# A TensorE order with an empty GpSimd instruction as the relay between two row tiles

## The chip, the cores and the metric

The kernel runs on one core of a Trainium2 chip. The metric is the device time of one execution in microseconds, median over runs. The engines are TensorE (PE, with its weight loads PEld), VectorE (DVE), ScalarE (ACT), GpSimd (POOL) and SyncE (SP, which issues most DMAs).

## What is computed

A token-wise gate mixes an attention block and a gated feed-forward block of the same input, in float32. There are 2048 tokens of width 512, 32 query heads of width 16 that share one key head and one value head, and a hidden width of 1376.

```python
g = sigmoid((x * gate_w).sum(-1, keepdims=True))
q = (x @ wq) split into 32 heads;  k = x @ wk;  v = x @ wv
a = concat_heads(softmax(q @ k.T * 16**-0.5) @ v) @ wo
b = (gelu(x @ w_gate) * (x @ w_up)) @ w_down
out = g * a + (1 - g) * b
```

## The kernel before

A first part (82 us) loads the inputs, computes keys, values and all queries, writes the queries to a scratch tensor in HBM, and does the first feed-forward chunks. Then comes one long stretch (1147 us) in which attention and feed-forward are interleaved on TensorE, and a short end (15.5 us) for the last output projection.

In the long stretch TensorE's program order is written out by hand, in `PLAN`: 78 lines, one for each feed-forward or output-projection job (the first line has none), with steps that `play` (called at the end of `mix_kernel`) turns into instructions:

- **S** and **Z**: one score pair (`scores`, L751): two matmuls on the two row tiles (rows 0 to 50 and 64 to 114 of the array), each 512 columns, into one PSUM area of two banks; then ScalarE's exp over 128x1024 into a buffer `p` (L754, 12 buffers). S uses area 0 or 1 in turn, Z uses area 2, which `z` of a job holds between H and R. There are 1024 of them.
- **V**: one step of probabilities times values (`pv`, L821): eight matmuls on four column tiles of 32, over all 128 rows. It needs the `p` of two scores. There are 512.
- **H**: opens a job with two accumulators, `z` in area 2 and `y` in a bank of its own.
- **F**: one pair of matmuls of the job (`pair_mm`, L519), one for z and one for y, 512 columns each, on the two row tiles of 64 rows at the same time. A gate job has 24 F (`gate_job`), a down job or output job 12, 18 or 24.
- **R**: closes the job and issues its VectorE work; **T** issues the tanh of the gelu on ScalarE.

A contraction over 128 rows is split over the two row tiles. In half 0 of a job z uses the rows 0 to 63 and y the rows 64 to 127; in half 1 they change places. So the bank of z passes from one row tile to the other in the middle of the job, and the matmuls of half 1 may not start before those of half 0 have ended. `pair_mm` secures that with a relay: an instruction on GpSimd (L527) that waits for the last F of half 0 and that the first F of half 1 waits for. The steps that stand in PLAN between the 12th and the 13th of 24 F run meanwhile. In the whole list the half change holds these steps:

| steps in the half change | jobs before |
|---|---|
| S V S | 43 |
| S V V S | 17 |
| S V V S S | 7 |
| others with V | 9 |
| S S | 1 |

`split` (L201, L202) divides weights and inputs into a high part (VectorE, L201) and a low part (GpSimd's subtraction, L202). Its work is put into `slot` calls between the F, and it shares GpSimd's queue with the relay. `score`, `visit`, `norm` and `advance` issue further loads, normalisation and gelu steps as the list goes on.

Of the kernel before, what the change touches and what calls it, by code (L numbers as in the profile page):

```python
# [9 lines left out]
F32 = mybir.dt.float32  # L10
# [10 lines left out]
S = 2048  # L21
D = 512
H = 32
DH = 16
F = 1376
# [17 lines left out]
PB = 12  # L43
PLAN = [
# [78 lines left out]
]  # L123


# [1 line left out]
def mix_kernel(ctx, tc, xT, wq, wo, wf, out):  # L127
    nc = tc.nc
    cp = ctx.enter_context(tc.tile_pool(name="cp", bufs=1))
# [363 lines left out]
    def slot(split_too):  # L493
        for q in (todo, lazy, bg) if split_too else (bg,):
            if q:
                return q.pop(0)()
# [7 lines left out]
            nc.tensor.matmul(ps, a, b, start=(first and q == 0), stop=(last and q == len(terms) - 1),  # L504
                             skip_group_check=True)

    mark = cp.tile([1, 1], F32, name="mark")
    SYNC = mybir.DependencyInfo(mybir.DependencyClass.Sync, mybir.DependencyReason.DATA)

    def after(ins, name):  # L510
        tc.add_manual_dep(ins, name, SYNC, reason="a bank passes from one row tile to the other")

    def pair_mm(z, y, X, Y):
        for half in range(2):
            for q in range(len(X)):
                for j, (ps, (a, b)) in enumerate(((z, X[q]), (y, Y[q]))):
                    lower = (j + half) % 2
                    rs = slice(64 * lower, 64 * lower + 64)
                    mm = nc.tensor.matmul(ps, a[rs], b[rs], start=(half == 0 and q == 0),  # L519
                                          stop=(half == 1 and q == len(X) - 1), skip_group_check=True)  # L520
                    if half == 1 and q == 0:
                        after(mm.ins, relay[0])
                    if half == 0 and q == 0 and j == 0:
                        behind = [None, None]
                    behind[j] = mm.ins.name
                if half == 0 and q == len(X) - 1:
                    relay = nc.gpsimd.memset(mark, 0.0).ins  # L527
                    for name in behind:
                        after(relay, name)
                    relay = [relay.name]  # L530
                if q % EVERY == EVERY - 1 and (half == 0 or q + 4 <= len(X)):
                    slot(half == 1 or q + 6 <= len(X))
                yield
# [403 lines left out]
```

## Time and profile before

| | |
|---|---|
| median of 3 runs | 1246.28 us (1244.94 to 1249.26) |
| profiled execution, its own time | 1246.9 us |
| span of its trace | 1244.8 us |
| TensorE, ScalarE, VectorE, GpSimd busy | 99%, 83%, 42%, 17% |
| granted TensorE clock, mean | 0.999 |

The page gives busy shares and the chain of work that ended last. TensorE's matmuls overlap, so that the sum of their durations is no measure; the prediction goes by differences of their starts, which the order of time shows to 0.01 us.

### The profile page before, as it was taken

What the parts mean: (1) busy time and instruction counts of PE and PEld (TensorE: products, weight loads), DVE (VectorE), ACT (ScalarE), POOL (GpSimd) and SP (SyncE); (2) the same over time, 40 slices, a digit from 0 to 9 for tenths busy, and PEclk for the clock granted to TensorE, in tenths of its full rate; (3) what the DMA queues carried; (4) which work ended last, traced back from release to release, by engine and by line L of the source; (5) the groups of instructions that cost most, each with busy time, mean ns of one, the idle gap of its engine ahead of it and who ended that gap; (6) DMA issues with size and microseconds to landing.
All of it is one profiled execution on the core that took longest, in us unless ns stands there. A gap on an engine that the chain in (4) does not pass through costs nothing.

```text
span 1244.8 us, 23618 instructions
## 1 busy us (share of the span) xinstructions
PE 1237.2 (99%) x9742; PEld 657.5 (53%) x9742; DVE 526.2 (42%) x844; ACT 1031.7 (83%) x1127; POOL 215.6 (17%) x265
## 2 busy tenths in 40 slices
PE   9999999999999999999999999999999999999998
PEld 6775555454544554545454555554544555455544
DVE  7872553525423144443443234162455126253334
ACT  5448888988888888888888788888889888898894
POOL 5420311212210120211230021120231011121100
PEclk9999999999999999999999999999999999999999
DMA  8541201103201211101210221010211201010000
GB/s 329 193 149 43 83 14 65 40 23 107 73 15 31 70 40 40 65 24 40 89 53 14 74 65 40 14 65 16 92 58 40 74 14 65 14 58 34 14 1 34
DMA packets 28317, 73.89 MB, mean 59 GB/s; under 512 B 4208, under 2 KB 4464, under 8 KB 28208
## 3 DMA queue, kind: packets, MB, share of 16 engines
q1 hardware_dynamic: 27664, 71.32, 17.1%
q8 instruction: 77, 1.26, 0.4%
q0 software_dynamic: 256, 0.79, 0.2%
q10 hardware_dynamic: 288, 0.26, 0.1%
q14 instruction: 32, 0.26, 0.1%
HBM read 57.41 MB, written 14.94 MB: 58 GB/s over the span
## 4 chain that ended last, share of the span: by engine, by line
PE 92%; issue 1%; POOL 0%; DVE 0%; ACT 0%; DMA 0%; SPq 0%; POOLq 0%
PE acc L821 38%; PE s L751 23%; PE y L519 17%; PE z L519 13%; PE wos L504 1%; POOL xl L202 0%; DVE acc L634 0%; DMA Q<-scr 0%; PE wof L504 0%; ACT p L754 0%; SPq L364 0%; ACT sq L551 0%; SPq L363 0%; POOLq L202 0%; POOL mark L527 0%
## 5 line engine op out<-in xcount | busy, mean ns | idle before, releaser
L754 ACT ACTIVATE p<-s 128x1024 f32<-128x1024 f32 x1024 | 977.4, 1026 | 150.3 <-PE s L751 139.7
L821 PE MATMUL acc<-p,v 128*32 128x512 f32 x4096 | 496.4, 599 | 0.0
L751 PE MATMUL s<-Q,kp 51*128 51x512 f32 x2048 | 397.2, 421 | 1.0 <-DMA Q<-scr 0.9
L751 PEld LDWEIGHTS s<-Q,kp 51*128 51x128 f32 x2048 | 183.7, 184 | 258.0 <-ACT p L754 167.3
L821 PEld LDWEIGHTS acc<-p,v 128*32 128x32 f32 x4096 | 106.7, 109 | 239.2 <-issue 231.2
L527 POOL MEMSET mark<- 1x1 f32 x77 | 7.6, 99 | 890.0 <-PE y L519 874.0
L519 PE MATMUL z<-xh,gh 64*128 64x512 f32 x312 | 122.9, 394 | 0.0
L519 PE MATMUL y<-xh,gh 64*128 64x512 f32 x312 | 122.8, 394 | 0.0
L519 PE MATMUL z<-xl,gh 64*128 64x512 f32 x312 | 122.2, 392 | 0.3 <-POOL xl L202 0.2
L519 PE MATMUL y<-xl,gh 64*128 64x512 f32 x312 | 122.4, 392 | 0.0
L544 DVE COPY gs<-z 128x512 f32<-128x512 f32 x39 | 27.0, 692 | 225.4 <-PE z L519 214.9
L519 PE MATMUL z<-xh,gl 64*128 64x512 f32 x312 | 121.9, 391 | 0.0
L519 PE MATMUL y<-xh,gl 64*128 64x512 f32 x312 | 121.9, 391 | 0.0
L202 POOL TENSOR_TENSOR gl<-st,gh 128x512 fp32r<-128x512 f32 x80 | 107.4, 1361 | 36.5 <-DVE gh L201 35.7
L624 DVE SCALAR_TENSOR_TENSOR acc<-z,gc,acc 128x512 f32<-128x512 f32 x24 | 18.0, 751 | 130.9 <-PE z L519 128.3
L519 PE MATMUL z<-dh,hh 64*128 64x512 f32 x176 | 69.2, 393 | 0.0
L519 PE MATMUL y<-dh,hh 64*128 64x512 f32 x176 | 69.1, 393 | 0.0
L519 PE MATMUL y<-dl,hh 64*128 64x512 f32 x176 | 68.9, 392 | 0.0
L519 PE MATMUL z<-dl,hh 64*128 64x512 f32 x176 | 68.9, 391 | 0.0
L519 PE MATMUL z<-dh,hl 64*128 64x512 f32 x176 | 68.8, 391 | 0.0
L519 PE MATMUL y<-dh,hl 64*128 64x512 f32 x176 | 68.7, 391 | 0.0
L519 PEld LDWEIGHTS y<-xh,gl 64*128 64x128 f32 x312 | 57.7, 185 | 8.4
(174 smaller groups left out, 1536.9 us busy)
## 6 DMA issues: line engine op xcount, KB each, us to landing
st<-wf SPq DMA_DIRECT2D x40, 768.0 KB
scr<-q SPq DMA_DIRECT2D x16, 512.0 KB
Q<-scr SPq DMA_DIRECT2D x64, 128.0 KB
Q<-scr SPq DMA_DIRECT2D x64, 64.0 KB
out<-acc SPq DMA_DIRECT2D x16, 256.0 KB
xr<-xT SPq DMA_DIRECT2D x6, 512.0 KB
xst<-xT SPq DMA_DIRECT2D x12, 256.0 KB
st<-wf SPq DMA_DIRECT2D x5, 256.0 KB
```

Source lines behind the costliest of these rows:

```text
L202: eng_l.tensor_sub(lo, src, hi)
L504: nc.tensor.matmul(ps, a, b, start=(first and q == 0), stop=(last and q == len(terms) - 1), skip_group_check=True)
L519: mm = nc.tensor.matmul(ps, a[rs], b[rs], start=(half == 0 and q == 0), stop=(half == 1 and q == len(X) - 1), skip_group_check=True)
L527: relay = nc.gpsimd.memset(mark, 0.0).ins
L544: nc.vector.tensor_copy(gs, g)
L624: nc.vector.scalar_tensor_tensor(o, ps, w, o, op0=ALU.mult, op1=ALU.add)
L751: nc.tensor.matmul(ps[:, j * TG : (j + 1) * TG], kp[rs, kc * P : (kc + 1) * P], Q[u][rs, pr], start=True, stop=True)
L754: nc.scalar.activation(p, ps, AF.Exp, bias=0.0, scale=SCALE)
L821: nc.tensor.matmul(accp[u][32 * j : 32 * j + 32], vt[:, kc], pb[s, j // 2][:, (j % 2) * TG : (j % 2 + 1) * TG], start=(kc == 0), stop=(kc ...
```

## The change

The relay's instruction becomes an empty one instead of a memset of one element, and the tile `mark`, which only the memset wrote, goes. Its dependencies stay as they are. Beside it all 77 job lines of PLAN are replaced by a new order of the same steps; five of them are shown here. A V group is a run of V with nothing between. In numbers: F 1608 and 1608, S and Z together 1024 and 1024 (119 Z before, 148 after), V 512 and 512, V groups 275 and 245. The half change holds S S in 52 jobs after, S V S in 13, one S in 5, and others with V in 7.

```diff
 PLAN = [
     "t: S2",
-    "f: H F6 S F3 S F3 S V S F S F5 S F3 S F3 R S V S Z T S V2 Z S V2 S",
-    "f: H F3 S F3 S F3 S V S F2 S F6 S F R S V2 S Z S V3 S",
-    "f: H F3 S F3 S F3 S V2 S F3 S F4 S F2 R S V2 S",
-    "f: H F S F5 S F3 S F3 S V S F3 S F3 S F3 S F3 R S V S Z T S V4 Z S2 V2 S",
-    "f: H F3 S F3 S F3 S F3 S V S F S F5 S F3 S F3 R S V Z S T S V4 S Z S V2 S",
...
+    "f: H F6 S F6 S2 F6 S F4 S F2 R S V S Z T S V3 Z S2 V2 S",
+    "f: H F3 S F3 S F3 S V S F S F6 S F2 R S V S Z S V3 S Z S V2 S",
+    "f: H F3 S F6 S2 F6 S F3 R S V S Z S V2 S",
+    "f: H F3 S F3 S F3 S F3 S V2 S F2 S F4 S F3 S F3 R S V Z S T S V4 S Z S V2 S",
+    "f: H F3 S F3 S F6 S2 F6 S F3 S F3 R S V Z S T S V4 S Z S V2 S",
...
 ]
...
-    mark = cp.tile([1, 1], F32, name="mark")
     SYNC = mybir.DependencyInfo(mybir.DependencyClass.Sync, mybir.DependencyReason.DATA)
...
                 if half == 0 and q == len(X) - 1:
-                    relay = nc.gpsimd.memset(mark, 0.0).ins
+                    relay = nc.gpsimd.nop(nofuse=True).ins
                     for name in behind:
                         after(relay, name)
                     relay = [relay.name]
```

144 rows, old and new, of the table PLAN are left out of this document.

## The prediction

> **What bounds the kernel now.** I read the page first: busy shares, granted clock, chain. Then the busy time by stretch, then the order of time on TensorE at single hand-overs, last the views of the GpSimd relay.
>
> ```profile
> span 1244.8 us, 23618 instructions
> ...
> PE 1237.2 (99%) x9742; PEld 657.5 (53%) x9742; DVE 526.2 (42%) x844; ACT 1031.7 (83%) x1127; POOL 215.6 (17%) x265
> ...
> PE 92%; issue 1%; POOL 0%; DVE 0%; ACT 0%; DMA 0%; SPq 0%; POOLq 0%
> PE acc L821 38%; PE s L751 23%; PE y L519 17%; PE z L519 13%; PE wos L504 1%; POOL xl L202 0%; DVE acc L634 0%; DMA Q<-scr 0%; PE wof L504 0%; ACT p L754 0%; SPq L364 0%; ACT sq L551 0%; SPq L363 0%; POOLq L202 0%; POOL mark L527 0%
> ```
> ```profile
> 0.00:82.20 82.20, 78.96 (x334) 60.61 (x334) 64.57 (x108) 35.84 (x62) 33.66 (x55) 1.00 0.63 233
> 82.20:1229.30 1147.10, 1146.67 (x9360) 587.98 (x9360) 450.60 (x717) 995.84 (x1065) 181.91 (x211) 1.00 0.15 47
> 1229.30:1244.80 15.50, 11.62 (x52) 8.94 (x48) 11.05 (x20) 0.00 (x0) 0.00 (x0) 0.94 0.18 68
> ```
>
> The chain lies 92% on TensorE. The second row of the stretches (columns: stretch, its length, then busy us of PE, PEld, DVE, ACT, POOL) is the part that PLAN orders: 1147.1 us, in which TensorE is without an instruction for 0.4 us, at full granted clock. The 82.2 us ahead of it and the 15.5 us behind it hold nothing that the diff touches. So the time is the sum of TensorE's steps in the list's order, and a new order is worth what it changes in the steps' prices. Busy time can't show those, since matmuls overlap; starts can. One hand-over of a gate job, TensorE alone:
>
> ```profile
> 142.15 0.40 PE L519 MATMUL z<-xh,gh 64*128 64x512 f32 x1
> ...
> 142.62 0.39 PE L519 MATMUL z<-xh,gl 64*128 64x512 f32 x1
> ...
> 142.85 0.41 PE L751 MATMUL s<-Q,kp 51*128 51x512 f32 x2
> 143.19 1.07 PE L821 MATMUL acc<-p,v 128*32 128x512 f32 x8
> 144.18 0.50 PE L751 MATMUL s<-Q,kp 51*128 51x512 f32 x2
> 144.52 0.39 PE L519 MATMUL y<-xh,gh 64*128 64x512 f32 x1
> ...
> 144.76 0.39 PE L751 MATMUL s<-Q,kp 51*128 51x512 f32 x2
> 144.99 0.39 PE L519 MATMUL y<-xl,gh 64*128 64x512 f32 x1
> ```
> ```profile
> 150.30 3.57 PE acc L821 x32
> ...
> 387.50 2.71 PE acc L821 x24
> ```
>
> An F is a pair z, y on the two row tiles, an S one score pair, a V eight matmuls on L821. Three F and their switch to S take 142.85 - 142.15 = 0.70, so 0.233 us each; S to F beside no V is 144.99 - 144.76 = 0.23. The second fence, pieces of the chain, has groups of four V and of three: a further V costs 3.57 - 2.71 = 0.86. Around a V group three steps are longer: S to V 143.19 - 142.85 = 0.34 (0.11 over 0.23); V to S 0.99 (0.13 over 0.86, and 3.57 - 4 x 0.86 gives the same 0.13); the S behind it 144.52 - 144.18 = 0.34 (0.11 over). **A V group costs 0.35 us beyond its work**, whatever its length.
>
> The check is the whole stretch. PLAN holds 1608 F, 1024 S (Z included), 512 V, and V stand in 275 groups. 2632 x 0.233 + 512 x 0.86 = 613.3 + 440.3 = 1053.6; the rest of the 1147.1 is 93.5 us, or 0.34 for each of 275 groups. So these prices explain the stretch, waits are a few us at most, and 0.34 is what I use (0.35 is rounding and a little of other waits the other way).
>
> **The list.** Counted in the diff: F, S and V are as many as before, V groups are 245 instead of 275. 30 x 0.34 = 10.2 us leave TensorE, on the path, with nothing to hide them. Where they come from: of the 77 jobs the half change (last F of half 0 to first F of half 1) holds V in 76 before, 43 of them S V S. After it holds S2 in 52, one S in 5, V in 20. The V taken out join groups elsewhere. Five V follow an F directly, which the trace doesn't show; between no surcharge and one more of 0.11 that is 0.5 us either way, and I take the price of S to V, as F and S cost each other nothing.
>
> **The hand-over.** S V S gives the relay 0.34 + 0.99 + 0.34 us, so none of those 76 is seen to stall. S2 gives 0.46 us. The trace has S2 once, with the memset:
>
> ```profile
> 817.06 0.39 PE L519 MATMUL z<-xh,gl 64*128 64x512 f32 x1
> ...
> 817.29 0.68 PE L751 MATMUL s<-Q,kp 51*128 51x512 f32 x4
> ...
> 817.58 0.15 POOL L527 MEMSET mark<- 1x1 f32 x1 [8.74 <-PE y L519]
> ...
> 817.78 0.18 PEld L519 LDWEIGHTS z<-xh,gh 64*128 64x128 f32 x1
> ...
> 817.81 0.47 PE L519 MATMUL y<-xh,gh 64*128 64x512 f32 x1
> ...
> 818.12 0.39 PE L519 MATMUL z<-xl,gh 64*128 64x512 f32 x1
> ```
> ```profile
> L527 POOL MEMSET mark<- x77: 88/88/381, 86.8 to 1219.2; 1x1 f32 x77
> L527 POOLq EVENT_SEMAPHORE  x76: 17/17/17, 101.5 to 1219.1; - x76
> its engine sat idle before it (us, times) until:
>   PE y L519: 874.0, 75
>   PE s L751: 15.9, 1
> ```
>
> The last pair of half 0 ends at 817.45. The memset starts 0.13 later, takes 0.15, and the weight load of half 1 goes 0.05 behind its end, at +0.33. Without a wait the second pair of half 1 would start at 817.29 + 2 x 0.23 + 0.23 = 817.99; it starts at 818.12. So a release at +0.33 costs 0.13 us, and the latest release that costs nothing is +0.20 after the end of half 0 (for one S: -0.03).
>
> The usual memset takes 0.088, so a release at +0.27 and 0.07 lost. Were the new relay as slow, 52 x 0.07 + 5 x 0.30 = 5.1 us of the 10.2 would go back. That is one end for the empty instruction. The other is from the first memset, the only one of 77 that has no EVENT_SEMAPHORE ahead of it (76 rows of it against 77):
>
> ```profile
> 86.35 0.40 PE L519 MATMUL y<-xh,gl 64*128 64x512 f32 x1
> ...
> 86.82 0.09 POOL L527 MEMSET mark<- 1x1 f32 x1 [4.09 <-PE y L519]
> ```
>
> It starts 0.07 behind the pair's end instead of 0.13. That first one has no earlier write of mark to wait for; the nop writes nothing, and so should have one wait as well. With a body of 0 to 0.02 (an EVENT_SEMAPHORE takes 0.017) and the 0.05 to TensorE the release comes at +0.12 to +0.14, ahead of +0.20: S2 costs nothing, a single S 0.15 to 0.17. I take this end, as the nop is nearer to the semaphore rows than to a memset that writes: 5 x 0.15 = 0.7 us. It can't gain below nothing, since the relay is off the path wherever the release is early.
>
> One doubt on that split: the Trainium skill, Perfetto Trace Analysis, section GPSIMD Engine Instruction, says that an instruction that reads no tensor has a single point of time reported, so where the memset begins within its 0.28 us isn't sure. By that the sum lies anywhere between 10.2 - 5.1 and 10.2 - 0.7, which are the ends already taken.
>
> Queued behind the waiting nop on GpSimd are the subtractions of the next weights (L202), and the next gate job's F wait for those. They queued behind EVENT_SEMAPHORE and memset likewise, so nothing is added. What moves with the S (the Q loads on SP, the slots of DVE work) comes as often as before; DMA is 15% busy in the stretch, DVE 451 of 1147 us. Without that cover one late split costs what it costs now at the second group's first gate job:
>
> ```profile
> L519 PE MATMUL z<-xl,gh 64*128 64x512 f32 x312 | 122.2, 392 | 0.3 <-POOL xl L202 0.2
> ```
>
> that is 0.3 us of idle TensorE in the whole run; I set the change at nothing.
>
> **Sum.** 10.2 - 0.7 = 9.5 us off the profiled span: 1244.8 to 1235.3. The profiled execution took 1246.9, the median of three runs is 1246.28, so the span lies 1.5 below the median. The same 9.5 off the median gives 1236.8.
>
> **Rivals.** *The relay stays as slow as a memset* (the nop keeps two waits, or costs as much to dispatch): 10.2 - 5.1, time 1241.2. For it: both go through the same queue. Against: one write and one wait less. Chance 0.13.
>
> *Scores come too dense, and ScalarE's exp holds the banks.*
>
> ```profile
> 626.48 0.39 PE L751 MATMUL s<-Q,kp 51*128 51x512 f32 x2
> ...
> 626.97 1.03 ACT L754 ACTIVATE p<-s 128x1024 f32<-128x1024 f32 x1 [0.26 <-PE s L751]
> ```
> ```profile
> 85.37 1.94 ACT L754 ACTIVATE p<-s 128x1024 f32<-128x1024 f32 x2
> ```
>
> A score's bank comes free 0.49 + 1.03 = 1.52 us after its start. In F3 S F6 S2 the second of the two S takes the bank of the S ahead of F6, 0.23 + 1.40 + 0.23 = 1.86 later: 0.34 to spare, if ScalarE isn't behind. It needs 1.94 - 1.03 = 0.91 per exp, and F3 S brings one every 0.93, so a backlog doesn't shrink there. 0.1 lost at each of 52 would make 5.2: time 1242.0. Against: V groups between lines, at 0.99 and more without a score, let it catch up, and it is busy 996 of 1147 us. Chance 0.08.
>
> *Slower: GpSimd is late.* The nop stands in order behind L202's subtractions, 1.36 us each:
>
> ```profile
> L202 POOL TENSOR_TENSOR gl<-st,gh 128x512 fp32r<-128x512 f32 x80 | 107.4, 1361 | 36.5 <-DVE gh L201 35.7
> ```
>
> With S V S a delay of a microsecond is free; with S2 it all falls on TensorE. A mean loss of 10.2 / 57 = 0.18 us over the 57 short hand-overs takes the gain away, one of 13.9 / 57 = 0.24 makes it slower by 0.3%; if every second one met half a subtraction, 57 x 0.5 x 0.68 = 19.4, time 1255.5. Against: GpSimd sat waiting for TensorE ahead of 76 of 77 memsets, and the first too had 4.09 us idle. The Trainium skill, PSUM — Partial Sum Buffer, section Engine vs sequencer instructions, counts a nop as handled by the sequencer, which waits for earlier work to be dispatched, not done; that would take even this delay away unless a wait on GpSimd's own work is put in. No run shows it yet. Chance 0.04.
>
> **How the numbers follow.** The forecast as it stands has 0.70, the rivals 0.13, 0.08 and 0.04, and 0.05 are left for what I don't see. A difference of 0.3% (3.7 us) is about what a measurement of this kernel can tell from no change. Faster by more: all of the forecast, two thirds of the first rival, half of the second, some of the rest, 0.86. Slower: the third rival and a little, 0.05. Within: 0.09. The range runs from 0.35 a group, no hand-over loss and the runs' own scatter (10.5 + 1.8, so 1234.0) to the two cheaper rivals (1242.0, with 0.8 of scatter 1242.8).
>
> **What would show it.** Right: the stretch from 82.2 on is 1137 to 1138 us long; V groups cost 0.34 as before; at S2 hand-overs half 1 starts 0.46 after the first S, within 0.02; TensorE still 99% busy, ScalarE 84%. First step wrong: groups other than 245, or longer steps around them. Second: the gap from S2 to the next F and the one behind it sum to 0.53 or more. Wrong altogether: S that follow the end of an exp by 0.05, or weight loads of L519 that wait for POOL L202.

## The result, and the profile after

The changed kernel takes 1235.8 us (median of 6 runs, 1235.4 to 1236.9) against 1246.0, a ratio of 0.9914 with a 95% interval of 0.9902 to 0.9925. The forecast was 1236.8. The lines of the page of the changed kernel that answer to those of before:

```profile
span 1233.6 us, 23557 instructions
...
PE 1226.2 (99%) x9742; PEld 663.6 (54%) x9742; DVE 519.9 (42%) x844; ACT 1028.3 (83%) x1127; POOL 206.9 (17%) x188
...
PE 91%; issue 1%; ACT 1%; DVE 0%; POOL 0%; DMA 0%; SPq 0%; POOLq 0%; ACTq 0%
```

TensorE is as full as before, with the same 9742 matmuls. The busy time by stretch (from the first score to the first matmul of the last projection, and what lies around it) says where the time went:

```profile
0.00:80.30 80.30, 77.87 (x334) 60.74 (x335) 61.12 (x108) 35.85 (x62) 33.77 (x55) 1.00 0.66 239
80.30:1218.40 1138.10, 1137.02 (x9360) 593.93 (x9360) 447.81 (x717) 992.45 (x1065) 173.10 (x134) 1.00 0.15 47
1218.40:1233.60 15.20, 11.30 (x52) 8.93 (x48) 10.98 (x20) 0.00 (x0) 0.00 (x0) 0.99 0.18 69
```

The ordered stretch is 9.0 us shorter (1147.1 to 1138.1), the first part 1.9, the end 0.3. So four fifths of the 11.2 us between the two profiled spans lie where the list acts; the other 2.2 lie where the prediction expected nothing. (The expectations below count the stretch to the last V, 0.9 less than these rows: 1146.2 before, 1137.2 after.)

A half change with S2 in the changed kernel, in order of time:

```profile
241.77 0.39 PE L518 MATMUL z<-xh,gl 64*128 64x512 f32 x1
...
242.00 0.62 PE L750 MATMUL s<-Q,kp 51*128 51x512 f32 x4
242.27 0.18 PEld L518 LDWEIGHTS z<-xh,gh 64*128 64x128 f32 x1
...
242.46 0.40 PE L518 MATMUL z<-xh,gh 64*128 64x512 f32 x1
...
242.70 0.39 PE L518 MATMUL z<-xl,gh 64*128 64x512 f32 x1
```

Half 1 starts 0.46 after the first S, and the next pair 0.24 later: no stall, where the memset of before cost 0.13. With one S in between the relay shows, and so does its time:

```profile
206.73 0.39 PE L518 MATMUL z<-xh,gl 64*128 64x512 f32 x1
...
206.96 0.39 PE L750 MATMUL s<-Q,kp 51*128 51x512 f32 x2
207.23 0.18 PEld L518 LDWEIGHTS z<-xh,gh 64*128 64x128 f32 x1 [0.31 <-POOLq L526]
...
207.57 0.39 PE L518 MATMUL z<-xl,gh 64*128 64x512 f32 x1
```
```profile
L526 POOLq EVENT_SEMAPHORE  x77: 17/17/17, 84.3 to 1213.8; - x77
its engine sat idle before it (us, times) until:
who waited for it (us, times):
  PEld z L518: 1.6, 5
```

Half 0 ends at 207.12, the weight load goes 0.11 later, and the second pair starts 0.15 late (207.57 instead of 206.96 + 2 x 0.23). The second view is that of the relay's line: all that the trace has of the empty instruction is a semaphore instruction of 17 ns, and TensorE waited for it only at the 5 half changes with one S.

### The profile page after: what moved, and what is told of

Same layout as the page of the kernel before. It is cut to its first block, busy times and chain, and to the rows that moved or that the text cites. A ratio compares the mean times of both kernels' runs of the same rounds, so it can differ in the third digit from the quotient of the medians.

```text
span 1233.6 us, 23557 instructions
## 1 busy us (share of the span) xinstructions
PE 1226.2 (99%) x9742; PEld 663.6 (54%) x9742; DVE 519.9 (42%) x844; ACT 1028.3 (83%) x1127; POOL 206.9 (17%) x188
## 4 chain that ended last, share of the span: by engine, by line
PE 91%; issue 1%; ACT 1%; DVE 0%; POOL 0%; DMA 0%; SPq 0%; POOLq 0%; ACTq 0%
PE acc L820 37%; PE s L750 23%; PE z L518 18%; PE y L518 12%; PE wos L504 1%; ACT p L753 1%; POOL xl L202 0%; DVE acc L633 0%; DMA Q<-scr 0%; PE wof L504 0%; SPq L364 0%; ACT sq L550 0%; DVE sq L547 0%; DVE sq L546 0%; DVE gs L543 0%
## 5 line engine op out<-in xcount | busy, mean ns | idle before, releaser
L820 PE MATMUL acc<-p,v 128*32 128x512 f32 x4096 | 490.2, 598 | 0.0
L750 PE MATMUL s<-Q,kp 51*128 51x512 f32 x2048 | 376.8, 418 | 1.4 <-DMA Q<-scr 1.1
L820 PEld LDWEIGHTS acc<-p,v 128*32 128x32 f32 x4096 | 110.7, 109 | 244.5 <-issue 236.0
L202 POOL TENSOR_TENSOR dl<-st,dh 128x512 fp32r<-128x512 f32 x44 | 57.6, 1310 | 54.7 <-PE s L750 26.5
L623 DVE SCALAR_TENSOR_TENSOR acc<-z,gc,acc 128x512 f32<-128x512 f32 x24 | 18.0, 750 | 109.1 <-PE z L518 80.3
L518 PEld LDWEIGHTS z<-xh,gh 64*128 64x128 f32 x312 | 58.0, 186 | 9.1 <-POOLq L526 0.9
```

The lines of the kernel that those rows point to most:

```text
L202: eng_l.tensor_sub(lo, src, hi)
L623: nc.vector.scalar_tensor_tensor(o, ps, w, o, op0=ALU.mult, op1=ALU.add)
L750: nc.tensor.matmul(ps[:, j * TG : (j + 1) * TG], kp[rs, kc * P : (kc + 1) * P], Q[u][rs, pr], start=True, stop=True)
L820: nc.tensor.matmul(accp[u][32 * j : 32 * j + 32], vt[:, kc], pb[s, j // 2][:, (j % 2) * TG : (j % 2 + 1) * TG], start=(kc == 0), stop=(kc ...
```

## The experiments

Results first. Each ratio is to the kernel before on the same chip, whose median there was 1246.0 to 1247.3, so ratios and stretches compare better than times do.

| run | time us | ratio (95%) | stretch by rows |
|---|---|---|---|
| before | 1246.0 | 1 | 1147.1 |
| changed | 1235.8 | 0.9914 (0.9902 to 0.9925) | 1138.1 |
| nop, old list | 1245.4 | 0.9985 (0.9976 to 0.9994) | 1147.1 |
| memset, new list | 1243.8 | 0.9973 (0.9963 to 0.9984) | 1143.7 |
| 35 more groups | 1247.2 | 0.9996 (0.9987 to 1.0005) | 1149.2 |
| one score | 1243.5 | 0.9968 (0.9956 to 0.9980) | 1145.2 |
| before again | 1245.4, one run | | 1146.9 |
| busy GpSimd, nop | 1235.5, one run | | 1138.0 |
| busy GpSimd, memset | 1273.2, one run | | 1174.7 |
| early split, two | 1235.4 | 0.9913 (0.9899 to 0.9926) | 1137.8 |
| early split, one | 1234.4 | 0.9898 (0.9883 to 0.9913) | 1136.9 |
| changed again | 1236.9 | 0.9918 (0.9904 to 0.9931) | 1138.3 |
| nop, old list again | 1244.8 | 0.9987 (0.9978 to 0.9996) | 1147.2 |

**Each part alone.** The nop with the old list:

```diff
-    mark = cp.tile([1, 1], F32, name="mark")
...
-                    relay = nc.gpsimd.memset(mark, 0.0).ins
+                    relay = nc.gpsimd.nop(nofuse=True).ins
```

> The old list of steps with the empty instruction as relay: one part of the change alone. Theory 'groups' (a V group costs 0.34 us beyond its work, and the gain is 30 groups fewer): the relay is off the path while S V S stands in the half change, so the time is that of before, 1246.0, within 0.5; only the one S2 half change gains 0.13. Rival 'relay' (the shorter relay itself brought the gain): 1236 to 1240.

```profile
80.70:1227.80 1147.10, 1146.70 (x9360) 589.24 (x9360) 450.02 (x717) 995.60 (x1065) 172.87 (x133) 1.00 0.15 47
```

The stretch hasn't moved, as theory 'groups' says. The time has, by 0.15%, more than the 0.5 us allowed; that is taken up with the first part below. The other part alone is the new list with the memset of before:

> The new list of steps with the memset as relay: the other part alone. Theory 'groups': 52 half changes with S2 lose 0.07 each, 5 with one S lose 0.30 instead of 0.14: 3.6 + 0.8 = 4.4 above the changed kernel, 1240.2, and the S2 half changes show a gap of 0.05 to 0.07 more in the step behind S2 or the one after. Rival 'relay': 1246. Rival 'scores' (ScalarE's pace and the banks set the time, relay and groups fall into slack): 1235.8.

```profile
81.40:1225.10 1143.70, 1142.25 (x9360) 589.97 (x9360) 448.81 (x717) 996.77 (x1065) 181.38 (x211) 1.00 0.15 47
```
```profile
114.82 0.63 PE L751 MATMUL s<-Q,kp 51*128 51x512 f32 x4
...
115.11 0.09 POOL L527 MEMSET mark<- 1x1 f32 x1 [11.99 <-PE y L519]
...
115.26 0.18 PEld L519 LDWEIGHTS z<-dh,hh 64*128 64x128 f32 x1 [0.23 <-POOL mark L527]
...
115.59 0.39 PE L519 MATMUL z<-dl,hh 64*128 64x512 f32 x1
```

5.6 us above the changed kernel in the stretch instead of 4.4: the usual S2 loses 0.08 (115.59 instead of 114.82 + 3 x 0.23 = 115.51), one with a memset of 0.16 loses 0.15, and two with a memset of some 0.36 lose 0.35. By the starts of the steps 5.0 of the 5.6 lie at the 57 short half changes. So the list alone gives 3.4 of the stretch's 9.0 us, the nop alone gives nothing there, and the other 5.6 need both: the nop pays only where V no longer covers the relay.

**The price of a group.** The new list with more, shorter groups and the same steps:

```diff
-... S2 V2 S ...
+... S V S V S ...      (35 places)
```

> The new list with the empty relay, where 35 line parts 'S2 V2 S' become 'S V S V S': the same F, S and V, 280 V groups instead of 245. Theory 'groups': 35 x 0.34 = 11.9 above the changed kernel, 1247.7. Rival 'scores': the same steps in nearly the same places, 1235.8 within 1.5. If single groups were dearer or cheaper than runs of two, the difference per group leaves 0.33 to 0.36.

```profile
81.50:1230.70 1149.20, 1148.33 (x9360) 587.74 (x9360) 447.63 (x717) 995.95 (x1065) 172.76 (x134) 1.00 0.15 47
```

11.1 us in the stretch, 0.32 per group, 0.01 under the range set; some waits went at the same time, since the stretch holds 0.5 to 0.7 us less of steps that start late. Single groups aren't cheaper: from the first V to the next S a lone V takes 0.996 us and a pair 0.882 + 0.972, so either has 0.14 over the 0.858 of a further V. The rival 'scores' is out. With this price 30 groups are worth 9.5 to 10.2.

**A shorter cover.** One S in place of two:

```diff
-... F6 S2 F6 ...
+... F6 S F S F5 ...      (52 places like this)
```

> The new list with the empty relay, where in the 52 half changes that hold S2 the second S moves behind the first F of half 1, so that one S is left to cover the relay. Theory 'groups' with a release 0.11 us after the end of half 0 (TensorE's weight load then needs 0.03 less than nothing to be free): each loses 0.14, 52 x 0.14 = 7.3, 1243.1. A relay that is quicker than its rows show: 1235.8 to 1238. A relay as slow as the memset: 52 x 0.30 = 15.6, 1251.4.

```profile
143.38 0.39 PE L518 MATMUL z<-xh,gl 64*128 64x512 f32 x1
...
143.62 0.40 PE L750 MATMUL s<-Q,kp 51*128 51x512 f32 x2
143.89 0.50 PE L518 MATMUL z<-xh,gh 64*128 64x512 f32 x1
...
144.23 0.39 PE L750 MATMUL s<-Q,kp 51*128 51x512 f32 x2
```

7.1 us in the stretch, 0.14 per place; in the rows the second S comes 0.15 late (144.23 instead of 143.62 + 0.46). So the relay's release is where the sum put it; one S is too short a cover, and two are enough.

**Does a busy GpSimd hold the relay up?** A subtraction without use goes ahead of each relay:

```diff
+    dum = cp.tile([P, TG], F32, name="dum")
+    nc.gpsimd.memset(dum, 0.0)
...
+                    if half == 0 and q == len(X) - 3:
+                        early = mm.ins.name
...
+                    after(nc.gpsimd.tensor_sub(dum, dum, dum).ins, early)
                     relay = nc.gpsimd.nop(nofuse=True).ins
```

> The changed kernel with one more subtraction of 128x512 on GpSimd ahead of each relay, which may start when the third last F of half 0 has ended, and so runs while half 0 ends. It computes nothing that is used. Theory 'ahead' (the empty instruction fires while GpSimd's engine still works): the relay comes at +0.04 as before, the stretch is 1137.2 to 1139 long. Rival 'in order' (GpSimd is late, the third rival of the prediction): the subtraction ends about 1.0 after half 0, each S2 loses 0.87 and each single S 1.10: 52 x 0.87 + 5 x 1.10 = 50.7, stretch 1188.

> The same busy GpSimd with the memset as relay. Both theories: the memset runs behind the subtraction, so each S2 loses about 0.95 and each single S 1.2: 52 x 0.95 + 5 x 1.2 = 55, stretch 1192. If it isn't longer than 1143 to 1145, the added subtraction doesn't fall into the half change and the run with the empty relay tells nothing.

The same half change with the nop, then with the memset:

```profile
241.94 0.39 PE L520 MATMUL z<-xh,gl 64*128 64x512 f32 x1
...
242.03 1.04 POOL L530 TENSOR_TENSOR dum<-dum 128x512 f32<-128x512 f32 x1 [10.56 <-PE y L520]
242.17 0.62 PE L755 MATMUL s<-Q,kp 51*128 51x512 f32 x4
242.44 0.18 PEld L520 LDWEIGHTS z<-xh,gh 64*128 64x128 f32 x1
...
242.63 0.40 PE L520 MATMUL z<-xh,gh 64*128 64x512 f32 x1
```
```profile
247.15 0.39 PE L521 MATMUL z<-xh,gl 64*128 64x512 f32 x1
...
247.24 1.04 POOL L531 TENSOR_TENSOR dum<-dum 128x512 f32<-128x512 f32 x1 [11.53 <-PE y L521]
247.39 0.62 PE L756 MATMUL s<-Q,kp 51*128 51x512 f32 x4
...
248.22 0.09 POOL L532 MEMSET mark<- 1x1 f32 x1
...
248.36 0.18 PEld L521 LDWEIGHTS z<-xh,gh 64*128 64x128 f32 x1 [0.78 <-POOL mark L532]
```

With the nop half 1 starts at 242.63, 0.46 after the first S, while the subtraction runs to 243.07. With the memset the weight load stands until 248.36. The stretches are 1138.0 and 1174.7: nothing against 36.6 us over the changed kernel's. The memset's price is under the 55 expected, as the subtraction took 1.04, not 1.36, and ended 0.74 after half 0 (248.28 against 247.54), not 1.0. In both runs it was still at work at all 57 short half changes. So a subtraction that runs doesn't hold the nop up, and the prediction's third rival is out; in the changed kernel itself GpSimd's engine was idle at all 57. A subtraction that still waits for its input in the queue ahead of the nop was not tried.

**The largest wait left.** In the changed kernel TensorE stands behind a split of x at the second token group's first gate job:

```profile
644.12 3.09 POOL L202 TENSOR_TENSOR xl<-xst,xh 128x512 fp32r<-128x512 f32 x2 [9.23 <-DVE xh L201]
...
646.15 0.39 PE L518 MATMUL z<-xh,gh 64*128 64x512 f32 x1
...
647.26 0.49 PE L518 MATMUL z<-xl,gh 64*128 64x512 f32 x1 [0.72 <-POOL xl L202]
```

`pair_mm` lets splits into half 0 only early in it (`q + 6 <= len(X)`), never in jobs of 12 F. Two versions let them in there too:

```diff
-                    slot(half == 1 or q + 6 <= len(X))
+                    slot(half == 1 or q + 6 <= len(X) or len(X) == 6)                # two
+                    slot(half == 1 or q + 6 <= len(X) or (len(X) == 6 and q == 2))   # one
```

> The changed kernel, where the jobs of 12 F may also split the next inputs in half 0 (in the others that is as it was). Theory: the largest wait left, 0.36 + 0.99 us behind POOL xl at 645 to 648, goes, since the four parts are then split ahead of the first gate job of the next token group: stretch 1135.9, time 1.3 below the changed kernel, 0.1%. Rival: the subtractions put in ahead of the relay wait for VectorE in GpSimd's queue and hold the relay up in 6 jobs by up to 0.5 each: stretch 1137 to 1139.

The wait went, but the stretch gained only 0.3. A new wait took its place:

```profile
915.20 0.43 DVE L201 CAST xh<-xst 128x512 fp32r<-128x512 f32 x1 [4.31 <-DMA xst<-xT]
915.55 0.75 DVE L623 SCALAR_TENSOR_TENSOR acc<-z,gc,acc 128x512 f32<-128x512 f32 x1
...
916.35 0.51 PE L750 MATMUL s<-Q,kp 51*128 51x512 f32 x2 [0.93 <-DVE acc L623]
```

VectorE's third cast stood in its queue waiting for the part's DMA, the reading of z stood behind the cast, and Z, which needs the area of z, behind that. The rival's mechanism (a relay held up) wasn't it: the short half changes lose what they lose in the changed kernel. With one split fewer:

> As the early split, but with one split in half 0 of a job of 12 F instead of two: no third part is asked of VectorE while its DMA is still on the way. Theory: both the wait behind POOL xl at 645 to 648 and the wait of Z behind VectorE at 916 are gone: stretch 1135.9, against 1137.2 of the changed kernel; time 1.3 below the changed kernel of the same chip. Rival: a relay that is held up by the subtraction ahead of it gives that back: 1137.

```profile
81.30:1218.20 1136.90, 1136.58 (x9360) 594.35 (x9360) 445.92 (x717) 992.29 (x1065) 172.98 (x134) 1.00 0.15 47
```

Both waits are gone; the stretch is 1.4 shorter than that of the changed kernel beside it (1138.3), as expected. At a ratio of 0.9898 this is the fastest version, though in time the intervals of the two still overlap (0.9883 to 0.9913 against 0.9904 to 0.9931).

**The first part.** Three runs bear on the 1.9 us that it was shorter:

> The kernel before once more, unchanged, for the part ahead of the hand-ordered stretch: its first score started at 82.24 us in the profile of before and at 80.33 in the changed kernel's, though nothing of the change lies there. Theory 'chance' (two engines met there differently in one execution): anywhere from 80.3 to 82.5, the stretch 1146.2 long again. Rival 'systematic' (the old order makes the first part longer): 82.2 again.

> The changed kernel once more, beside the others of this call: ratio to before 0.9914 within 0.001, stretch 1137.2 within 0.2. Its first score starts anywhere from 80.3 to 82.5 if the first part's length is chance.

> The old list with the empty instruction once more: its stretch was as long as before's (1146.2), yet its runs were 0.15% faster. Theory 'end and start': the end is 0.25 shorter without the memset (16.05 against 16.30) and the rest is the first part's scatter: ratio 0.9998 to 0.9990. Rival 'systematic': 0.9985 again, with a first score near 80.7 where before has 82.

The first score starts at 82.2 and 81.0 in two profiles of the kernel before, at 80.3 and 81.7 in two of the changed one, at 80.7 and 80.2 with the nop and the old list. So single executions differ by more than a microsecond. (The changed kernel's second ratio, 0.9918, is within the 0.001; its stretch up to the last V, 1137.5, is 0.3 above 1137.2 instead of at most 0.2.) One cause shows: in the first profile of before, VectorE's subtraction ran beside two of GpSimd's and took 3.02 us, and TensorE waited for it,

```profile
40.46 1.36 POOL L416 TENSOR_TENSOR hl<-gsf,hh 96x512 fp32r<-96x512 f32 x1
...
40.59 3.02 DVE L202 TENSOR_TENSOR xl<-xr,xh 128x512 fp32r<-128x512 f32 x1
...
41.77 1.28 POOL L202 TENSOR_TENSOR dl<-st,dh 128x512 fp32r<-128x512 f32 x1
...
43.66 0.50 PE L389 MATMUL gf<-xl,gh 128*128 128x512 f32 x1 [0.84 <-DVE xl L202]
```

where in the second it came earlier and took

```profile
40.17 0.67 DVE L202 TENSOR_TENSOR xl<-xr,xh 128x512 fp32r<-128x512 f32 x1
```

The nop with the old list was 0.13% to 0.15% faster in two series, 1.6 to 1.9 us, so not all is chance, and a steady part shows too. Ten matmuls in a row of one kind in the first part, in the second profile of before, then in the changed kernel:

```profile
63.99 0.40 PE L261 MATMUL pq<-xl,wqh 128*128 128x512 f32 x1
...
66.09 0.40 PE L261 MATMUL pq<-xl,wqh 128*128 128x512 f32 x1
```
```profile
63.97 0.39 PE L261 MATMUL pq<-xl,wqh 128*128 128x512 f32 x1
...
66.01 0.39 PE L261 MATMUL pq<-xl,wqh 128*128 128x512 f32 x1
```

Nine steps take 2.10 us with the memset and 2.04 with the nop. Over 285 steps of the first part (without the 15 around that wait) this makes 0.98 us (65.03 against 64.05), and each of the two sums is the same within 0.03 in all profiles: four of kernels with the memset, nine with the nop, whatever the list. The granted clock is 1.00 in both kernels' rows of this part. Some of it is lost again in the wait for the first Q (0.8 and 0.9 us in the profiles of before, 1.0 to 1.5 in four with the nop). The end is 0.25 shorter in the same way (16.05 from the last V on, against 16.30). Why, in a part that runs ahead of the first relay, stays open: the memset and its tile `mark` were never taken apart. These two make at most 1.2 of the 1.6 to 1.9 us; the rest was not settled.

## Why the prediction was right

- **What bounds.** Right: the price list of F, S, V and groups explains the stretch before and after, and the run with 35 more groups moved by their price.
- **The list.** 30 groups at 0.34 gave 10.2; the measured price of 0.32 to 0.34 gives 9.5 to 10.2. The five V that follow an F directly cost what a V behind an S costs (0.33 us from the F to the V), as was taken.
- **The hand-over.** The release was put at +0.12 to +0.14 and came at +0.11; a single S was put at 0.15 and lost 0.15; S2 at nothing, and 46 of 52 lost nothing. The other six are the second rival in small: the second score waited for its bank, 0.05 to 0.07 in five and 0.40 in the first job. Both ends of the bound turned up in runs: 0.7 us with the nop, some 5.6 more with the memset, where 4.4 had been the difference.
- **A late split "set at nothing".** Mis-sized: the wait behind POOL xl grew from 0.86 us, with the pair behind each, to 1.35. With the banks and some small ones the late starts in the stretch sum to some 4.2 us against 2.2 before, which would have left 8.2 of the 10.2. The stretch gave 9.0, since F behind F came 0.2320 us apart instead of 0.2328, some 1100 times; no term of the prediction has that gain, and its cause stays open.
- **"The first part and the end hold nothing that the diff touches."** This step failed: with the nop the first part's matmuls take 0.98 us less in every profile, the end takes 0.25 less, and the runs of the nop with the old list put the whole at 1.6 to 1.9 us. The median came out 10.2 lower instead of 9.5 since this and the stretch's shortfall have opposite signs; that the total was nearer than its parts is luck.
- **Rivals.** The relay as slow as a memset: out, the kernel with the memset shows what that would have been. Dense scores: seen at six of the 52 half changes, 0.75 us in all instead of 5.2. GpSimd late: out by the busy runs, for a subtraction that runs. The Trainium skill, PSUM — Partial Sum Buffer, section Engine vs sequencer instructions, had it that a nop is done by the sequencer without waiting for the engine; the two busy runs agree (0 against 36.6 us).

## What to carry to other kernels

Where TensorE never idles, price the switches of its order by differences of starts, count them in the old and the new order, and check that the prices sum up to the whole stretch before believing the difference. Where an instruction only passes a signal on, try one that writes nothing: here the next weight load went 0.11 us behind the signal with it and some 0.28 with the memset, and it didn't wait for a subtraction that ran on its engine (so it is no sign that such work is done). But it pays only where its latency is exposed, so change the cover along with it. A wait that goes may uncover one queued behind it on another engine: look at what stands in that queue before moving work forward.

## What was not expected of the hardware

The nop overtook a subtraction that was still running on the same engine by 0.6 us (weight load at 242.44, end of the subtraction at 243.07), at no cost. An instruction of VectorE took 3.02 us instead of 0.67 beside two of GpSimd (1.36 and 1.28) that followed each other, so it ended behind both, and TensorE lost 0.84 us waiting for it, 0.07% of the run. And matmuls far ahead of the first relay took 1.5% longer where the relay was a memset (65.03 against 64.05 us for 285 steps), for a reason that is not known.
